# Starting a fused state-space and gated-MLP kernel tile by tile: first weights on two rings, ten f-tiles of the first token block ahead

## The chip, the cores and the metric

One NeuronCore of a Trainium2 chip. The metric is the device time of one execution in microseconds (us); lower is better. Every timed kernel is run several times, in rounds with the kernel before on the same chip.

## The reference, cut to what matters

```python
x = A_x                                   # (1, 2048, 576) bf16
xn = layernorm(x)                         # over the 576 columns
A  = s5(xn, Lambda, B, C, log_dt) + xn * Dskip    # linear recurrence over 2048 steps, 576 states
g, u = xn @ w_gate, xn @ w_up             # (2048, 576) @ (576, 4608), twice
Bm = (sigmoid(g) * u) @ w_down            # (2048, 4608) @ (4608, 576)
return x + A + Bm
```

Nearly all the work is matmul. The kernel cuts the 2048 tokens into four blocks of 512 (each four token tiles of 128 rows), and the 4608 columns f into 36 f-tiles of 128, twelve of them a "slot". A *group* is the gate and up product of one f-tile and one block: 18 matmuls of 512 columns. ScalarE (ACT) evacuates a group with a sigmoid and a cast, VectorE (DVE) multiplies the two into hT.

## The kernel before

TensorE needs normalized, transposed tokens (xT) and the first weights before it can do anything of its own; until then it multiplies zeros to keep its clock up. The first four token tiles come through the rings (queues of transfers) of SyncE (SP) and ACT, everything else through GpSimd (POOL).

```python
    def load_x(tt, eng, tag=None):
        if tag is None:
            xt = lnp.tile([P, D], BF16, name="xt", bufs=8)
        else:
            xt = hpool.tile([P, D], BF16, name="xt0", tag=tag, bufs=10)
        eng.dma_start(xt[:], x[tt * P:(tt + 1) * P, :])
        xts[tt] = xt
# ...
    def load_wgu(key, eng_g, eng_u):
        f0 = (key[0] % NC * (FC // FP) + key[1]) * FP * P
        w = wpool.tile([P, NH, FP * P], BF16, name="wgu", bufs=4)
        fs = slice(f0, f0 + FP * P)
        for (eng, rows, src) in ((eng_g, slice(0, H), B_w_gate), (eng_u, slice(H, P), B_w_up)):
            eng.dma_start(w[rows, :, :], src[:, fs].rearrange("(c p) f -> p c f", p=H))
        wgu_t[key] = w
# ...
    for tt in range(TT_B):
        load_x(tt, nc.sync if tt % 2 == 0 else nc.scalar)
    for pr in range(2):
        load_wgu((0, pr), nc.gpsimd, nc.gpsimd)
    for tt in range(TT_B, 2 * TT_B):
        load_x(tt, nc.gpsimd, "hst")
    dskip_rows = consts.tile([P, D], BF16, name="dskip_rows")
    nc.gpsimd.dma_start(dskip_rows[:], A_Dskip.partition_broadcast(P))
    for pr in range(2, 4):
        load_wgu((0, pr), nc.gpsimd, nc.gpsimd)
```

The first two groups, both on block 0, are done in halves of 256 columns, two token tiles to a half, transposed on TensorE:

```python
    for tt in range(2):
        ln_stats(tt)
        ln_std(0, tt, tt + 1)
    for tt in range(2):
        ln_recip(0, tt, tt + 1)
        ln_norm(tt, twice=False)
        start_transpose(tt)
    busy(20, P)
    start_copy(0, slice(0, NH), nc.scalar.copy)
    ln_stats(2)
    start_copy(1, slice(0, 5), nc.scalar.copy)
    ln_std(0, 2, 3)
    ln_stats(3)
    ln_std(0, 3, 4)
    start_copy(1, slice(5, NH), nc.vector.tensor_copy)
    for tt in range(2, TT_B):
        ln_recip(0, tt, tt + 1)
        ln_norm(tt, twice=False)
    start_groups[0].mms(slice(0, 2 * P))
    start_transpose(2)
    start_transpose(3)
    start_groups[1].mms(slice(0, 2 * P))
    for tt in range(2, TT_B):
        start_copy(tt, slice(0, 5), nc.scalar.copy)
        start_copy(tt, slice(5, NH), nc.vector.tensor_copy)
    for g in start_groups:
        g.mms(slice(2 * P, TB))
```

Then come six more groups of block 0, and then block 1, whose tokens are normalized on DVE in the background and transposed by DMA:

```python
            if slot == 0:
                order = [(f, 0) for f in range(2, 8)] + [(f, 1) for f in range(0, 8)]
                order += [(f, nb) for nb in range(2) for f in range(8, 12)]
# ...
            if slot == 0:
                run_groups([GateUp(slot, f, nb) for (f, nb) in order[:6]])
                catch_up_ln(1)
                order = order[6:]
                side_loads.extend([load_consts] + bt_loads)
            run_groups([GateUp(slot, f, nb) for (f, nb) in order])
```

## Time and profile before

| | before |
|---|---|
| median of 3 first runs (all 6 of the later comparison) | 509.69 us (509.9) |
| span of the profiled run, granted clock | 508.4 us, 1.00 |
| TensorE's first own matmul | 8.63 us |
| T2: first matmul on 512 columns, so both start groups' 256-column halves are done | 13.91 us |
| hole before block 1 | 1.79 us |
| first output matmul (pd) | 58.71 us |
| last matmul's start | 504.17 us |

Starts are counted from the beginning of the span. TensorE is busy without a gap from block 1's first group on, so whatever the start gains or loses appears unchanged at the end. The prediction shows TensorE's own lines. One more view: ACT's timeline of the kernel before. The columns are start, duration, engine (ACTq is its sequencer, issuing transfers), line, operation, output and input, count, and in brackets the idle time before and what ended it.

```profile
0.74 0.90 ACTq L139 DMA_DIRECT2D xt<-in_A_x_dram  x2
1.67 1.28 ACT L224 ACT_TABLE_LOAD   x1 [1.67 <-PEq L866]
4.69 0.29 ACT L224 ACTIVATE rstd<-mv,eps_t 128x1 f32<-128x1 f32 x1 [1.74 <-DVE mv L221]
```

ACT issues two token tiles, loads its square-root table, and then waits 1.74 us for DVE's statistics.

### The profile page before, as it was taken

The numbers are of one execution on the slowest core, as the hardware profiler recorded it, in microseconds if no ns is written. First come the engines' busy times: TensorE is split into PE (matmuls) and PEld (weight loads), VectorE is DVE, ScalarE is ACT, GpSimd is POOL, SyncE is SP. The second block draws the span as 40 slices with busy tenths as digits, with TensorE's granted clock in tenths as the row PEclk, the third lists the DMA queues.
The fourth block names the chain that finished last, engine by engine and source line by source line (L and its number), as shares of the span: only waits on it lengthen the run. The fifth ranks groups of instructions, "written<-read, shape, count | busy, mean of one in ns | idle before, by whom it ended". The sixth has DMA issues, their size and how long they took to land.

```text
span 508.4 us, 10667 instructions
## 1 busy us (share of the span) xinstructions
PE 500.6 (98%) x4536; PEld 292.6 (58%) x4536; DVE 323.5 (64%) x703; ACT 204.6 (40%) x368; POOL 96.6 (19%) x143
## 2 busy tenths in 40 slices
PE   8989999999999999999999999999999999999996
PEld 5445676444477444467764444774444774446775
DVE  6964999977888587868688667786675222221111
ACT  4757642556500756530016655005655005553000
POOL 6147430133110043110001231100431001300000
PEclk9999999999999999999999999999999999999999
DMA  8997997075220098342340662200753201600001
GB/s 208 172 170 143 235 194 125 2 164 122 57 57 25 1 170 153 76 107 69 73 104 3 163 141 48 46 24 1 150 122 81 48 25 38 172 1 4 33 25 36
DMA packets 42960, 45.60 MB, mean 90 GB/s; under 512 B 30496, under 2 KB 34336, under 8 KB 42912
## 3 DMA queue, kind: packets, MB, share of 16 engines
q0 software_dynamic: 12672, 34.23, 31.7%
q1 hardware_dynamic: 29808, 10.33, 10.2%
q8 instruction: 35, 0.57, 0.5%
q10 hardware_dynamic: 432, 0.37, 0.2%
q14 instruction: 13, 0.11, 0.1%
HBM read 34.36 MB, written 2.36 MB: 72 GB/s over the span
## 4 chain that ended last, share of the span: by engine, by line
PE 94%; DVE 3%; DMA 1%; ACT 1%; issue 0%
PE pgu L488 52%; PE pd L562 35%; PE pbu L517 7%; DVE bnst L220 1%; DMA xT<-xn 1%; DVE xn L240 1%; DMA xt<-in_A_x_dram 1%; ACT xT L737 0%; DVE acc L263 0%; PE ptr L734 0%; DVE mv L221 0%; DVE tmpxd L260 0%; DVE hT L497 0%; DVE ob L571 0%; DVE xn L245 0%
## 5 line engine op out<-in xcount | busy, mean ns | idle before, releaser
L488 PE MATMUL pgu<-xT,wgu 64*128 64x512 bf16 (+1 forms) x2628 | 283.7, 373 | 1.8 <-DMA xT<-xn 1.8
L488 PEld LDWEIGHTS <-wgu 64*128 64x128 bf16 x2628 | 130.0, 94 | 150.7 <-issue 2.5
L562 PE MATMUL pd<-wd,hT 128*128 128x288 bf16 x1152 | 144.6, 286 | 0.0
L494 ACT ACTIVATE sT<-pgu 128x512 bf16<-128x512 f32 x144 | 86.5, 600 | 119.4 <-PE pgu L488 109.7
L562 PEld LDWEIGHTS <-hT 128*128 128x128 bf16 x1152 | 112.2, 98 | 30.7 <-issue 0.8
L497 DVE TENSOR_TENSOR hT<-sT,uT 128x512 bf16<-128x512 bf16 x144 | 60.5, 421 | 100.0 <-ACT uT L495 99.8
L495 ACT CAST uT<-pgu 128x512 bf16<-128x512 f32 x144 | 84.1, 584 | 0.0
L151 POOL DMA_DIRECT2D wgu<-in_B_w_gate_dram x36 | 27.7, 769 | 227.7 <-PE pgu L488 207.7
L523 ACT COPY bure<-pbu 128x512 f32<-128x512 f32 x16 | 9.4, 585 | 104.3 <-PE pbu L517 88.5
L157 POOL DMA_DIRECT2D wd<-in_B_w_down_dram x36 | 26.4, 735 | 100.6 <-PE pd L562 99.5
L582 DVE TENSOR_TENSOR acc<-acc,pd 128x576 f32<-128x576 f32 x32 | 23.9, 750 | 24.1 <-PE pd L562 24.1
L579 DVE TENSOR_TENSOR ob<-acc,pd 128x576 bf16<-128x576 f32 x15 | 11.3, 754 | 40.9 <-PE pd L562 40.9
L517 PE MATMUL pbu<-xT,bt 64*128 64x512 bf16 x288 | 33.7, 376 | 0.0
L562 PEld LDWEIGHTS <-hst 128*128 128x128 bf16 x288 | 28.2, 98 | 7.1
L151 POOL DMA_DIRECT2D wgu<-in_B_w_up_dram x36 | 26.7, 742 | 1.5 <-issue 0.8
L562 PE MATMUL pd<-ctre,hst 128*128 128x288 bf16 x128 | 26.6, 286 | 0.0
L562 PE MATMUL pd<-ctim,hst 128*128 128x288 bf16 x128 | 26.6, 286 | 0.0
L432 DVE TENSOR_TENSOR_SCAN gre<-r,g0re,wrim 128x512 bf16<-128x512 f32 x20 | 25.5, 1277 | 0.1
L517 PEld LDWEIGHTS <-bt 64*128 64x128 bf16 x288 | 13.7, 94 | 17.1 <-issue 0.9
L439 DVE TENSOR_TENSOR_SCAN gim<-r,g0im,wrim 128x512 bf16<-128x512 f32 x16 | 20.4, 1276 | 0.0
L220 DVE BATCH_NORM_STATS2 bnst<-xt 128x6 f32<-128x288 bf16 x32 | 12.5, 433 | 2.4 <-DMA xt<-in_A_x_dram 2.4
L419 DVE TENSOR_TENSOR tq<-T,buim 128x512 bf16<-128x512 bf16 x20 | 13.7, 684 | 0.0
(113 smaller groups left out, 273.9 us busy)
## 6 DMA issues: line engine op xcount, KB each, us to landing
wgu<-in_B_w_gate_dram POOLq DMA_DIRECT2D x36, 288.0 KB, 4.4
wgu<-in_B_w_up_dram POOLq DMA_DIRECT2D x36, 288.0 KB, 5.1
wd<-in_B_w_down_dram POOLq DMA_DIRECT2D x36, 288.0 KB, 6.2
out_dram<-ob SPq DMA_DIRECT2D x15, 144.0 KB, 1.8
xt<-in_A_x_dram SPq DMA_DIRECT2D x10, 144.0 KB, 2.6
xt<-in_A_x_dram POOLq DMA_DIRECT2D x4, 144.0 KB, 7.2
bt<-ctre POOLq DMA_DIRECT2D x2, 288.0 KB, 6.9
bt<-ctim POOLq DMA_DIRECT2D x2, 288.0 KB, 7.8
```

The source lines that it names most:

```text
L151: eng.dma_start(w[rows, :, :], src[:, fs].rearrange("(c p) f -> p c f", p=H))
L157: nc.gpsimd.dma_start(wd[:], B_w_down[f0:f0 + FP * P, :].rearrange("(n p) d -> p n d", p=P))
L220: nc.vector.bn_stats(st[:, gi, :], xt[:, gi * DH:(gi + 1) * DH])
L432: nc.vector.tensor_tensor_scan(gre[:], r_bc, w[:, 0, :], g0re[:, col], ALU.mult, ALU.add)
L439: nc.vector.tensor_tensor_scan(gim[:], r_bc, w[:, 1, :], g0im[:, col], ALU.mult, ALU.add)
L488: nc.tensor.matmul(self.ps[:, gi, cols], w[rows, c, fs], xT[self.nb][rows, c, cols], start=c == 0, stop=c == NH - 1)
L494: nc.scalar.activation(sT[:], self.ps[:, 0, :], ACT.Sigmoid)
L495: nc.scalar.copy(uT[:], self.ps[:, 1, :])
L497: nc.vector.tensor_mul(h[:], sT[:], uT[:])
L517: nc.tensor.matmul(out, w, xT[self.nb][rows, c, ts_], start=c == 0, stop=c == NH - 1)
L562: nc.tensor.matmul(out, lhsT, rhs[:, a * DH:(a + 1) * DH], start=i == 0, stop=i == n - 1)
L582: nc.vector.tensor_add(halves(acc[:]), halves(acc[:]), pd[:, :, 0:DH])
```

## The change

The intent: get the first weights in sooner by using both fast rings for them at once; let TensorE begin when one token tile is ready instead of two; and put ten groups of block 0 ahead of block 1, so that block 1's input has two groups' time more. The transfers that are not needed at once are held back by a small memset. The diff, cut to its core:

```diff
-    def load_wgu(key, eng_g, eng_u):
+    def load_wgu(key, eng_g, eng_u, held=False):
...
-        w = wpool.tile([P, NH, FP * P], BF16, name="wgu", bufs=4)
+        if key == (0, 4):
+            w = consts.tile([P, NH, FP * P], BF16, name="wgu4", tag="T1")
...                                       # T1's own tile is made later, in tables()
+        else:
+            w = wpool.tile([P, NH, FP * P], BF16, name="wgu", bufs=4)
+        if held:
+            nc.vector.memset(w[:, 0, 0:2], 0.0)
...
     for tt in range(TT_B):
         load_x(tt, nc.sync if tt % 2 == 0 else nc.scalar)
-    for pr in range(2):
-        load_wgu((0, pr), nc.gpsimd, nc.gpsimd)
+    load_wgu((0, 0), nc.sync, nc.scalar)
     for tt in range(TT_B, 2 * TT_B):
-        load_x(tt, nc.gpsimd, "hst")
+        load_x(tt, nc.sync, "hst")
+    for pr in range(1, 3):
+        load_wgu((0, pr), nc.sync, nc.scalar)
...                                       # pairs 3 and 4 and dskip: on gpsimd, in load_behind(), called later
-    wgu_next = [4]
+    wgu_next = [5]
-            prefetch_wgu(pairs_done[0] + 4)
+            prefetch_wgu(max(pairs_done[0] + 4, min(pairs_done[0], 4) + 5))
-            if side_loads and i % 3 == 2:
+            if side_loads and i % 3 == 1:
...                                       # the start, shortened: four tiles, one at a time
-    start_groups[0].mms(slice(0, 2 * P))
-    start_transpose(2)
-    ...
-    start_groups[1].mms(slice(0, 2 * P))
+    start_norm(0)
+    start_transpose(0)
+    busy(14, P)
+    start_copy(0, CA, nc.scalar.copy)
+    ...
+    start_copy(0, CB, nc.scalar.copy)
+    ...
+    for g in range(2):
+        start_mms(g, 0, range(0, 5))
+    start_norm(1)
+    start_transpose(1)
+    ...                                   # each start_mms: 128 columns of one tile
...
-                order = [(f, 0) for f in range(2, 8)] + [(f, 1) for f in range(0, 8)]
-                order += [(f, nb) for nb in range(2) for f in range(8, 12)]
+                order = [(f, 0) for f in range(2, 10)] + [(f, 1) for f in range(0, 10)]
+                order += [(f, nb) for nb in range(2) for f in range(10, 12)]
...
+                bg.add(0.0, lambda: want_bu(0))
+                bg.add(0.0, lambda: want_bu(1))
                 for i in range(len(chain)):
                     queue_ssm(i)
-                want_bu(0)
-                want_bu(1)
```

More of the change, by code (lines that the diff above doesn't have):

```diff
@@ L163, with load_behind @@
         load_x(tt, nc.sync if tt % 2 == 0 else nc.scalar)
-    for pr in range(2):
-        load_wgu((0, pr), nc.gpsimd, nc.gpsimd)
+    load_wgu((0, 0), nc.sync, nc.scalar)
     for tt in range(TT_B, 2 * TT_B):
-        load_x(tt, nc.gpsimd, "hst")
+        load_x(tt, nc.sync, "hst")
+    for pr in range(1, 3):
+        load_wgu((0, pr), nc.sync, nc.scalar)
     dskip_rows = consts.tile([P, D], BF16, name="dskip_rows")
-    nc.gpsimd.dma_start(dskip_rows[:], A_Dskip.partition_broadcast(P))
-    for pr in range(2, 4):
-        load_wgu((0, pr), nc.gpsimd, nc.gpsimd)
+    def load_behind():
+        for pr in range(3, 5):
+            load_wgu((0, pr), nc.gpsimd, nc.gpsimd, held=pr == 3)
+        nc.gpsimd.dma_start(dskip_rows[:], A_Dskip.partition_broadcast(P))
     eps_t = consts.tile([P, 1], FP32, name="eps_t")
@@ L210, with ln_stats @@
     ln_count = [0]
-    def ln_stats(tt):
+    bnst = {}
+    def ln_stats(tt, parts=(0, 1)):
         nb, tl = divmod(tt, TT_B)
-        if tl == 0:
+        if tl == 0 and 0 in parts:
             mvs[nb] = lnp.tile([P, TT_B, nc.vector.BN_AGGR_DIM], FP32, name="mv")
@@ L217, in ln_stats @@
         xt = xts[tt]
-        st = lnp.tile([P, 2, BN], FP32, name="bnst")
-        for gi in range(2):
+        if 0 in parts:
+            bnst[tt] = lnp.tile([P, 2, BN], FP32, name="bnst")
+        st = bnst[tt]
+        for gi in parts:
             nc.vector.bn_stats(st[:, gi, :], xt[:, gi * DH:(gi + 1) * DH])
-        nc.vector.bn_aggr(mvs[nb][:, tl, :], st[:])
+        if 1 in parts:
+            nc.vector.bn_aggr(mvs[nb][:, tl, :], st[:])
     def ln_std(nb, t0, t1):
@@ L309 @@
     c512, s512 = sc4[:, 3, :], sc4[:, 2, :]
-    T1 = consts.tile([P, NU, TB], BF16, name="T1")
+    T1 = None
     T2 = consts.tile([P, NU, TB], BF16, name="T2")
@@ L378, in tables @@
     def tables(pt, part):
+        nonlocal T1
+        if T1 is None:
+            T1 = consts.tile([P, NU, TB], BF16, name="T1", tag="T1")
         sb_, cb_ = sc_tab[(pt, 0)], sc_tab[(pt, 1)]
@@ L481, in open, with mms @@
             self.ps = ps_pair("pgu")
-        def mms(self, cols=slice(0, TB)):
+        def mms(self, cols=slice(0, TB), cs=range(NH)):
             w = wgu_t[(self.slot, self.f // FP)]
             fs = slice((self.f % FP) * P, (self.f % FP + 1) * P)
-            for c in range(NH):
+            for c in cs:
                 for gi, rows in ((0, slice(0, H)), (1, slice(H, P))):
@@ L737, in start_copy, with start_mms, start_norm @@
         eng(xT_tile(0)[:, cs, tt * P:(tt + 1) * P], ptrs[tt % 2][:, cs, :])
-    for tt in range(2):
-        ln_stats(tt)
-        ln_std(0, tt, tt + 1)
-    for tt in range(2):
+    def start_mms(g, tt, cs=range(NH)):
+        start_groups[g].mms(slice(tt * P, (tt + 1) * P), cs)
+    CA, CB = slice(0, 5), slice(5, NH)
+    def start_norm(tt):
         ln_recip(0, tt, tt + 1)
         ln_norm(tt, twice=False)
-        start_transpose(tt)
-    busy(20, P)
-    start_copy(0, slice(0, NH), nc.scalar.copy)
-    ln_stats(2)
-    start_copy(1, slice(0, 5), nc.scalar.copy)
-    ln_std(0, 2, 3)
-    ln_stats(3)
-    ln_std(0, 3, 4)
-    start_copy(1, slice(5, NH), nc.vector.tensor_copy)
-    for tt in range(2, TT_B):
-        ln_recip(0, tt, tt + 1)
-        ln_norm(tt, twice=False)
-    start_groups[0].mms(slice(0, 2 * P))
-    start_transpose(2)
-    start_transpose(3)
-    start_groups[1].mms(slice(0, 2 * P))
-    for tt in range(2, TT_B):
-        start_copy(tt, slice(0, 5), nc.scalar.copy)
-        start_copy(tt, slice(5, NH), nc.vector.tensor_copy)
-    for g in start_groups:
-        g.mms(slice(2 * P, TB))
+    ln_stats(0)
+    ln_std(0, 0, 1)
+    ln_stats(1, (0,))
+    start_norm(0)
+    start_transpose(0)
+    busy(14, P)
+    start_copy(0, CA, nc.scalar.copy)
+    ln_stats(1, (1,))
+    ln_std(0, 1, 2)
+    start_copy(0, CB, nc.scalar.copy)
+    ln_stats(2, (0,))
+    for g in range(2):
+        start_mms(g, 0, range(0, 5))
+    start_norm(1)
+    start_transpose(1)
+    start_copy(1, CA, nc.scalar.copy)
+    for g in range(2):
+        start_mms(g, 0, range(5, NH))
+    load_behind()
+    ln_stats(2, (1,))
+    ln_std(0, 2, 3)
+    start_copy(1, CB, nc.scalar.copy)
+    ln_stats(3, (0,))
+    start_norm(2)
+    start_mms(0, 1)
+    start_transpose(2)
+    start_mms(1, 1)
+    ln_stats(3, (1,))
+    ln_std(0, 3, 4)
+    start_copy(2, CA, nc.scalar.copy)
+    start_copy(2, CB, nc.scalar.copy)
+    start_norm(3)
+    start_mms(0, 2)
+    start_transpose(3)
+    start_mms(1, 2)
+    start_copy(3, CA, nc.scalar.copy)
+    start_copy(3, CB, nc.vector.tensor_copy)
+    for g in range(2):
+        start_mms(g, 3)
     for tt in range(TT_B, 2 * TT_B):
@@ L813 @@
             if slot == 0:
-                run_groups([GateUp(slot, f, nb) for (f, nb) in order[:6]])
+                run_groups([GateUp(slot, f, nb) for (f, nb) in order[:8]])
                 catch_up_ln(1)
-                order = order[6:]
+                order = order[8:]
                 side_loads.extend([load_consts] + bt_loads)
```

## The prediction

> **What bounds the kernel now.** I read the page first, then the TensorE part of the timeline, then the waits of the first 35 us, the chain of the first 30 us, GpSimd's timeline and a table by stretches. From the page, the busy line of TensorE and the head of the chain that ended last:
>
> ```profile
> PE 500.6 (98%) x4536; PEld 292.6 (58%) x4536; DVE 323.5 (64%) x703; ACT 204.6 (40%) x368; POOL 96.6 (19%) x143
> ...
> PE 94%; DVE 3%; DMA 1%; ACT 1%; issue 0%
> ```
>
> TensorE is busy for 98% of the span, so all that can be won is its idle time and its work that isn't the kernel's. The timeline of TensorE alone (start, duration, what, then what ended the idle time before) shows where that lies:
>
> ```profile
> 1.25 4.16 PE L726 MATMUL pgu<-warm 128*128 128x512 bf16 x16 [1.25 <-DVE warm L178]
> 6.13 1.23 PE L734 MATMUL ptr<-ident,xn 128*64 128x128 bf16 x36 [0.72 <-DVE xn L245]
> 7.29 1.29 PE L726 MATMUL pgu<-warm 128*128 128x128 bf16 x20
> 8.63 1.16 PE L488 MATMUL pgu<-xT,wgu 64*128 64x256 bf16 x18
> 9.79 1.23 PE L734 MATMUL ptr<-ident,xn 128*64 128x128 bf16 x36
> 10.95 14.78 PE L488 MATMUL pgu<-xT,wgu 64*128 64x256 bf16 x162
> 27.52 20.68 PE L488 MATMUL pgu<-xT,wgu 64*128 64x512 bf16 x190 [1.79 <-DMA xT<-xn]
> ```
>
> Two things are to be seen. The first matmul of the kernel's own work is at 8.63 us. And there is one hole afterwards, 1.79 us before 27.52, where block 1's first group waits for block 1's transposed input. From 27.52 to the last matmul, at about 504.5, the waits of TensorE list nothing. So the change can only act before 27.52; a prediction is a prediction of when the same amount of group work has been done there. The table by stretches (us; busy of TensorE and of its weight loads, DVE, ACT, POOL; clock, DMA share, GB/s) cuts that part:
>
> ```profile
> 10.95:14.07 3.12, 3.12 (x60) 2.75 (x58) 2.58 (x8) 3.08 (x5) 2.31 (x6) 1.00 1.05 286
> 14.07:25.74 11.67, 11.65 (x108) 5.06 (x104) 11.06 (x25) 8.08 (x14) 0.17 (x3) 1.00 0.98 170
> 25.74:27.52 1.78, 0.00 (x1) 0.03 (x1) 1.75 (x5) 1.21 (x3) 0.00 (x0) 1.00 0.89 132
> ```
>
> 108 matmuls, six groups of 18, take 11.65 us: 1.94 us for a full group. The 162 matmuls from 10.95 are three half groups (256 columns) and these six, so a half group takes (14.78 - 11.65) / 3 = 1.04 us and the two start groups are done at **14.07** (call this time T2). Block 1 waits, in the chain, behind DVE and then a transfer:
>
> ```profile
> 16.93 3.21 DVE xn L240 x4
> ...
> 23.07 4.31 DMA xT<-xn
> ```
>
> Weights are nearly as late as the input. GpSimd's queue has eight transfers out and issues the next when an old one has landed; the ends of its waits give the landings of the first two weight pairs:
>
> ```profile
> 7.40 0.54 POOL L169 DMA_DIRECT2D dskip_rows<-in_A_Dskip_dram  x1 [0.67 <-DMA wgu<-in_B_w_gate_dram]
> 8.86 0.77 POOL L151 DMA_DIRECT2D wgu<-in_B_w_gate_dram  x1 [0.93 <-DMA wgu<-in_B_w_up_dram]
> 10.35 0.76 POOL L151 DMA_DIRECT2D wgu<-in_B_w_up_dram  x1 [0.72 <-DMA wgu<-in_B_w_gate_dram]
> ```
>
> So gate 0 came at about 7.4, up 0 at about 8.8 (first used at about 8.6), gate 1 at about 10.3: one 288 KB piece each 1.5 us, near 200 GB/s.
>
> **What the skill says.** The Trainium skill, page "DMA: Bandwidth & Descriptors", section "Issuing engines are not separate DMA queues": all queues end on the same 16 DMA engines, and issuing from several saves only the sequencer's time. The trace agrees: DMA share is 0.89 to 1.05 in all these stretches. Two rings will not bring more bytes; they only change the order. Same page, "Queues, rings and completion order": each engine takes turns between rings. No run here shows that yet, but it means that a load behind others in its ring also shares with the other rings. The page "Perfetto Trace Analysis", section "DMA Instruction — HWDGE (DVE, Sync)": the issuing sequencer is held until its descriptors are made. Here a token tile (128 rows) held ACT for about 0.43 us; a weight piece has 64 x 9 = 576 runs of 512 bytes, a cost which this trace doesn't show. The page "TensorE: Matmul & The Clock Gate", section "Back-to-back issue gap": at small N the weight load also sets the spacing. The trace agrees in kind: a pair at 512 columns takes 1.94/9 = 216 ns, at 256 columns 116 ns and not 108.
>
> **The change, part by part.**
>
> *Ten f-tiles ahead.* Block 1 starts after ten groups of block 0, not eight. Its input, ready at about 27.5, is then needed only at T2 + 8 x 1.943 = T2 + 15.54. The kernel before would have done the same ten groups' work by 27.52 + 2 x 1.943 = 31.41. So if there is no hole,
>
> change of time = T2(after) + 15.54 - 31.41 = T2(after) - 15.87.
>
> With T2 kept at 14.07 the gain is the whole hole, 1.8 us.
>
> *One tile at a time.* I walk the new order with the durations of before. Tile 0: stats 3.6 to 4.65, root 0.29 on ACT, reciprocal and norm to 5.6 (6.07 for the first pair before: 6.13 was its first transpose), 18 transposes 0.61 to 6.25, ACT's five-chunk copy 0.70 to 7.07. So first own matmuls at 7.1 instead of 8.63, if gate 0 and up 0 are there: 4 x 147 KB of tokens and 2 x 295 KB of weights, 1.18 MB at some 200 GB/s from about 1.5 us, is 7.4; I take 7.1 to 7.6. Tile 1's root now stands on ACT behind that copy (7.0 to 7.3), so its norm ends at 7.9 and its transposes at 8.55, where before both first tiles were transposed by 7.36. Tile 2: copy of tile 1 9.4, root 9.6, norm 10.2, transposes 10.4 to 11.0, as before. Tile 3: its transposes stand on TensorE behind group 0's piece of tile 2, which waits for both copies of tile 2 (about 12.3): 12.65 to 13.25, where before it was 11.0. Copies to 14.05, then two pieces.
>
> *128-column pieces.* 8 pieces take the place of 4 halves. If a pair of 128-column matmuls costs 65 to 90 ns (transposes went at 34 ns each, 68 a pair; half of 116 is 58), a piece is 0.6 to 0.8 us, 0.7 in the middle: 8 x 0.7 = 5.6 against 1.16 + 3.12 = 4.3, so 1.3 us more TensorE work. Lower bound for T2: 7.4 + 3 x 0.61 + 5.6 = 14.8. By the walk: 14.05 + 2 x 0.7 = 15.45. I take **T2 = 15.3**, from 14.3 to 16.5. The earlier first matmul (1.2 to 1.5 us) is thus more than paid back.
>
> *Two rings, held loads.* Order of bytes: tokens 0 to 3 and pair 0, then tokens 4 to 7 and pairs 1 and 2, with pairs 3 and 4 from about 8.5. Pair 1 is needed at T2. Before gate 1 is in, about 2.36 MB must come plus what the other rings take, some 0.5 MB. The transfers of before had moved 2.8 MB by 13.5 and 3.1 MB by 15 (summed from GB/s by slice). So gate 1 lands at 14 to 15: just in time.
>
> *Rest.* The memset (59 ns for the small ones now) and the shifted side loads lie off the path. The state matmuls are asked for after the tables instead of at once; TensorE has other groups to do and has no wait there now: 0.
>
> Sum: 15.3 - 15.87 = -0.6 us, by T2 between -1.6 and +0.6. From 509.69 this is 509.1; I lean 0.1 further, since my walk charges every wait in full: **509.0 us**.
>
> **The rivals.** (1) *The full intent*: pieces overlap well, T2 stays near 14, gain 1.8 us, 507.9. For it: all instruction counts on DVE and ACT stay nearly the same. Against it: the bound of 14.8 has no waits in it. More than 2 us needs T2 below 13.9; only much cheaper pieces would do that. (2) *ACT's queue becomes the wait*: three weight issues on ACT before its 1.28 us table load (at 1.67 now). At 0.5 us each the table is in at 4.4, before the root is asked for at 4.65; at 0.9 us it is 5.6 and everything moves by 1 us, T2 = 16.3, 510.1. If a full ring holds ACT until bytes have moved, it could be 2 us. (3) *Weights become the wait*: the ring of SP carries tokens 4 to 7 ahead of gate 1, and three rings share from 8.5. With equal shares gate 1 could come at 16 to 17: 509.8 to 510.8. (4) *The hole moves but stays*: DVE begins block 1's statistics after tile 3's last copy, 13.8 instead of 12.18, so block 1's input comes at about 27.5 + 1.6 = 29.1, later if pairs 3 and 4 crowd the transposing transfers. It is needed at 30.8: 1.7 us to spare, so most likely hidden. A late evacuation of a PSUM buffer at the fifth or sixth group is tight by some 0.4 us in the same walk and could add as much.
>
> **Range and chances.** Rivals 2 and 3 add up to 1 or 1.5 us, rival 1 takes away 1.1; run-to-run spread was 508.88 to 510.46. So 507.3 to 510.9 for 8 in 10. Two per cent is 10 us, more than the whole start phase can give: reaching it by gain would need nearly all of the first 8.6 us gone, by loss a stall that no row hints at.
>
> **What would show it.** Right: no wait on DMA in front of the first block-1 matmul; first own matmul at 7.1 to 7.8; the 128-column groups at 0.6 to 0.8 us for 18; the first 512-column group at about 15.3; the rest as before. Wrong: the first full group near 14 (the pieces overlap) or past 16.5 with ACT's issues or a weight transfer named in front; a wait before block 1 again; or any TensorE idle time after 31 us, which would mean that moving the state matmuls mattered.

## The result, and the profile after

| | before | after |
|---|---|---|
| median, 6 runs each | 509.9 us | 518.29 us (518.04 to 518.95) |
| span and granted clock of the profiled run | 508.4 us, 1.00 | 516.3 us, 0.993 |
| first root on ACT | 4.69 | 11.57 |
| first own matmul | 8.63 | 15.29 |
| T2 | 13.91 | 23.45 |
| hole before block 1 | 1.79 | none |
| first output matmul | 58.71 | 66.55 |
| last matmul's start | 504.17 | 512.63 |

The ratio is 1.0169, with an interval of 1.0155 to 1.0182: slower by 8.4 us, which is within 2% and far outside the predicted range. (A ratio is the mean time of one kernel's fast runs over that of the other's in the same rounds, so it is not quite the ratio of the medians that are quoted.) Executions over 1.5% slower than the fastest of the same kernel are left out of the means.

From the page of the kernel after, TensorE's busy line and the head of the chain that ended last:

```profile
PE 503.6 (98%) x4602; PEld 295.3 (57%) x4602; DVE 323.3 (63%) x702; ACT 205.9 (40%) x371; POOL 90.3 (17%) x133
...
PE 91%; DVE 4%; ACT 2%; DMA 2%; issue 1%; SPq 0%; ACTq 0%
```

TensorE's share still reads 98%, and its busy time grew by just 3 us. The share of the chain that is TensorE's fell from 94 to 91%: work of others now stands in front of it. The timeline of TensorE shows where:

```profile
1.25 4.62 PE L744 MATMUL pgu<-warm 128*128 128x512 bf16 x16 [1.25 <-DVE warm L188]
12.58 1.17 PE L752 MATMUL ptr<-ident,xn 128*64 128x128 bf16 x18 [6.72 <-DVE xn L260]
13.69 1.68 PE L744 MATMUL pgu<-warm 128*128 128x128 bf16 x14
15.29 0.80 PE L506 MATMUL pgu<-xT,wgu 64*128 64x128 bf16 x20
...
22.27 18.01 PE L506 MATMUL pgu<-xT,wgu 64*128 64x128 bf16 x188 [0.17 <-ACT xT L755]
```

The zeros end at 5.87, and then TensorE stands still for 6.72 us, until the first normalized tile. After 22.27 it runs through what was the hole. The name behind the wait, DVE's xn, is only the last link. ACT's timeline holds the cause:

```profile
1.68 8.57 ACTq L157 DMA_DIRECT2D wgu<-in_B_w_up_dram  x3
10.27 1.28 ACT L239 ACT_TABLE_LOAD   x1 [10.27 <-DMA wgu<-in_B_w_gate_dram]
11.57 0.29 ACT L239 ACTIVATE rstd<-mv,eps_t 128x1 f32<-128x1 f32 x1
```

Three issues of weights take ACT's sequencer from 1.68 to 10.25. The same view in two narrow windows (1.7 to 3 and 9.63 to 10.3) takes them apart:

```profile
1.68 1.38 ACTq L157 DMA_DIRECT2D wgu<-in_B_w_up_dram  x2
...
9.64 0.60 ACTq L157 DMA_DIRECT2D wgu<-in_B_w_up_dram  x1
```

Two issues took 1.38 us together and the third 0.60 us of its own. Between 3.06 and 9.64 ACT's sequencer did nothing at all: it waited 6.58 us before the third issue. This is no issue cost. The waits list it only at the table load behind it, and for its whole 10.3 us. The Trainium skill, page "Perfetto Trace Analysis", section "DMA Instruction — HWDGE (DVE, Sync)", has the semaphore wait of such an instruction ahead of its use of the descriptor generator, and the trace agrees in that the wait is not part of the 0.60 us. What ended it stands in the chain of the first 45 us (start, duration, what):

```profile
1.66 7.96 DMA wgu<-in_B_w_gate_dram
9.64 0.60 ACTq L157
10.24 0.03 issue
10.27 1.28 ACT L239
11.57 0.30 ACT rstd L239
```

The landing of gate 0, the first weight piece on the *other* ring, at 9.62 us, releases ACT. And SP's queue has the same kind of wait, one issue later in order (from the waits of SP's queue, first 40 us; total, times, longest):

```profile
SPq L157 <- DMA wgu<-in_B_w_up_dram: 2.6, 1, 2.6
```

The built program says why. In it, every transfer issued by SP or ACT reports its landing on one of eight completion semaphores (counters by which engines tell each other that something is done) that the two engines use together, in turn; a ninth transfer takes the first one's semaphore and is issued only when that first one has landed. GpSimd has eight of its own. This is how the program was built; no run here shows it to be a limit of the chip. The turn follows the order of the built program, which is not that of the source: up 1, twelfth in the source, is the eighth there. So the 13th issue is up 2, on ACT, and the fifth is gate 0; the 14th is gate 2, on SP, and the sixth is up 0. These are the two waits that the trace shows. The kernel before had only four transfers on these two rings at the start, so it did not get round to a ninth there. ACT, which needs its sequencer for the table load and the root, is the wrong engine to be held.

The clock adds to it. The table by stretches (busy of TensorE, its weight loads, DVE, ACT, POOL; clock, DMA share, GB/s):

```profile
12.50:13.75 1.25, 1.17 (x19) 1.00 (x20) 0.93 (x4) 0.00 (x0) 0.00 (x0) 0.50 1.17 189
13.75:15.36 1.61, 1.61 (x17) 1.41 (x18) 0.61 (x4) 1.36 (x3) 0.00 (x0) 0.50 0.43 75
15.36:16.09 0.73, 0.73 (x23) 0.63 (x24) 0.69 (x3) 0.00 (x0) 0.42 (x1) 0.92 0.05 11
```

After the 6.7 us idle the granted clock is 0.50 until about 15.5. The Trainium skill, page "TensorE: Matmul & The Clock Gate", section "Part 1: The HAM clock gate (the "warmup" mystery)", has a clock that falls to half when TensorE was idle over an activity window and comes back after about 3.4 us of work; the trace agrees in kind (6.7 us idle, half clock, full again after 2.9 us of work, from 12.58 to about 15.5).

Last, one small new wait at the first output matmuls (TensorE's timeline from 60 to 75 us):

```profile
66.55 2.87 PE L580 MATMUL pd<-wd,hT 128*128 128x288 bf16 x22
69.86 5.32 PE L580 MATMUL pd<-wd,hT 128*128 128x288 bf16 x42 [0.45 <-DVE hT L515]
```

So the account is: T2 later by 23.45 - 13.91 = 9.54, hole gone 1.79, new wait 0.45: +8.2, against +8.46 at the last matmul's start and +8.4 in the timed runs.

### The profile page after: what moved, and what is told of

The parts are those of the page before. It is cut to its first block, busy times and chain, and to the rows that moved or that the text cites. A ratio compares the mean times of both kernels' runs of the same rounds, so it can differ in the third digit from the quotient of the medians.

```text
span 516.3 us, 10801 instructions
## 1 busy us (share of the span) xinstructions
PE 503.6 (98%) x4602; PEld 295.3 (57%) x4602; DVE 323.3 (63%) x702; ACT 205.9 (40%) x371; POOL 90.3 (17%) x133
## 3 DMA queue, kind: packets, MB, share of 16 engines
q10 hardware_dynamic: 2208, 1.25, 1.0%
## 4 chain that ended last, share of the span: by engine, by line
PE 91%; DVE 4%; ACT 2%; DMA 2%; issue 1%; SPq 0%; ACTq 0%
PE pgu L506 50%; PE pd L580 34%; PE pbu L535 7%; DMA wgu<-in_B_w_gate_dram 2%; DVE sctab L336 1%; DVE bnst L234 1%; DVE rnd L335 1%; DVE ang L360 1%; PE ptr L752 0%; ACT L512 0%; ACT xT L755 0%; DVE hT L515 0%; ACT uT L513 0%; PE pgu L744 0%; ACT L339 0%
## 5 line engine op out<-in xcount | busy, mean ns | idle before, releaser
L506 PEld LDWEIGHTS <-wgu 64*128 64x128 bf16 x2700 | 132.1, 94 | 149.1 <-issue 2.3
L515 DVE TENSOR_TENSOR hT<-sT,uT 128x512 bf16<-128x512 bf16 x144 | 60.7, 423 | 100.3 <-ACT uT L513 100.1
L157 POOL DMA_DIRECT2D wgu<-in_B_w_gate_dram x33 | 25.4, 771 | 245.1 <-PE pgu L506 191.3
L535 PE MATMUL pbu<-xT,bt 64*128 64x512 bf16 x288 | 33.7, 377 | 0.0
L157 POOL DMA_DIRECT2D wgu<-in_B_w_up_dram x33 | 24.5, 741 | 0.6 <-DMA wgu<-in_B_w_up_dram 0.6
```

The lines of the kernel that those rows point to most:

```text
L506: nc.tensor.matmul(self.ps[:, gi, cols], w[rows, c, fs], xT[self.nb][rows, c, cols], start=c == 0, stop=c == NH - 1)
L515: nc.vector.tensor_mul(h[:], sT[:], uT[:])
L535: nc.tensor.matmul(out, w, xT[self.nb][rows, c, ts_], start=c == 0, stop=c == NH - 1)
```

## The experiments

Theory: ACT is held by a completion semaphore that comes round after eight transfers (about 6.9 us of the loss), the cold clock adds about 1, and the tile-by-tile start costs the rest. Rivals: ACT's ring has no room for a fifth transfer, so ACT is held until bytes have moved; the weights themselves come late and would have held TensorE anyway; the ten f-tiles or the shifted background work cost time later. Twelve kernels ran; all gave the right result. Two more builds went to no chip: the change with the two state matmuls asked for at once as before (the schedule deadlocks while it is being built), and ten f-tiles ahead without the shifted side loads (reading a tile before it was written). So these two parts of the diff belong to the ten f-tiles and are no tuning of their own.

### u2_on_sp: take the held issue off ACT

```diff
-    for pr in range(1, 3):
-        load_wgu((0, pr), nc.sync, nc.scalar)
+    load_wgu((0, 1), nc.sync, nc.scalar)
+    load_wgu((0, 2), nc.sync, nc.sync)
```

> The changed kernel with one issue moved: up 2 from ACT's queue to SP's. My theory: ACT was held from 3.05 to 9.64 us by this one issue, which waits for a completion semaphore that gate 0 (landed at 9.62) still holds. Then ACT's table load is over at about 4.4 us, the first root starts at about 4.7 instead of 11.57, and the first own matmul waits for gate 0 only, at about 9.7 instead of 15.29. T2 comes down from 23.6 to 16.5 to 17.5 and the time to about 511.5 us (510.5 to 512.5). Rival: the three rings and late weights are the cause and ACT's wait only stood in front of them; then T2 stays above 21 us and the time above 515.5 us.

Measured: 514.52 us (4 runs; before 510.06), ratio 1.0098 [1.0071, 1.0125]. ACT's timeline:

```profile
3.08 1.28 ACT L239 ACT_TABLE_LOAD   x1 [3.08 <-issue]
4.73 0.29 ACT L239 ACTIVATE rstd<-mv,eps_t 128x1 f32<-128x1 f32 x1 [0.37 <-DVE mv L236]
```

With the third issue gone from ACT the root is back at 4.73 and T2 falls from 23.45 to 17.4. The time fell by less, because of TensorE's waits (total, times, longest):

```profile
PE pgu L506 <- DMA wgu<-in_B_w_up_dram: 1.6, 1, 1.6
PE pgu L506 <- DMA wgu<-in_B_w_gate_dram: 1.4, 1, 1.4
...
PE pd L580 <- DVE hT L515: 1.0, 1, 1.0
```

Gate 0 now holds the first own matmul to 8.86, and up 2, issued on SP at 9.47 and landed only at 23.2, holds TensorE for 1.58 us at 23.25. I had left that second one out. The mechanism was as expected, the size was not.

### x_on_pool: the same five transfers on ACT, fewer on the two rings together

```diff
     for tt in range(TT_B, 2 * TT_B):
-        load_x(tt, nc.sync, "hst")
+        load_x(tt, nc.gpsimd, "hst")
```

> The changed kernel with token tiles 4 to 7 issued by GpSimd instead of SP; ACT keeps its three weight issues. There are then ten transfers on SP and ACT at the start instead of fourteen, and up 2 waits for the semaphore of token tile 1 (landed at about 3.5 us), not of gate 0. My theory (completion semaphores): ACT is free at about 4.1, the table is in at 5.4, the root starts then, gate 0 lands before 8.5 because no tokens share its ring; T2 15 to 17 and 509.5 to 511.5 us. Rival (ring capacity: an issue is held until its ring has room, whatever the semaphores): ACT is still held until 8 to 10 us, as its ring has the same five transfers, and the time stays at 515 to 518.5 us.

Measured: 515.68 us (512.96 to 517.23, 4 runs, with granted clocks of 0.993 to 0.999), ratio 1.0106 [1.0066, 1.0146]; span of the profiled run 511.1. ACT's timeline:

```profile
1.67 2.60 ACTq L157 DMA_DIRECT2D wgu<-in_B_w_up_dram  x3
4.30 1.28 ACT L239 ACT_TABLE_LOAD   x1 [4.30 <-DMA xt<-in_A_x_dram]
```

ACT issues the very same five transfers (two tokens, three weights) and is free at 4.27, not 10.25. A ring too small for them would have held it here too, so the rival of the full ring is out. With four transfers fewer in the turn, up 2 is the tenth and has to wait for the second only, an early token tile: the releaser named is a token tile. The time was expected lower: gate 0 and up 0 came at about 9.1 and 9.6, T2 was 17.77, and some runs had a colder clock. The median lies in the rival's range of 515 to 518.5, so the time alone would not decide; ACT's row does. The spread makes this run good for the mechanism and poor for the time.

### ten_ahead: the ten f-tiles alone, on the kernel before

The diff's parts for ten f-tiles (tile wgu4 in T1's place, pair 4 on GpSimd behind pair 3, the prefetch rule, the two orders of ten, the state matmuls and side loads), with the start and the rings as before.

> The kernel before with the ten f-tiles ahead alone (with the buffer, side loads and order of the state matmuls that it needs), its start as it was. My theory: T2 stays at 14.1, the 1.79 us hole in front of block 1 closes, minus up to 0.4 us for a new wait of the first output matmul on hT: 508.1 to 508.6 us. Rival: the fifth pair's load makes block 1's transposed input later, or DVE falls behind so far that a wait of the same size opens elsewhere: 509.5 us or more.

Measured: 509.14 us (the median of three fast runs, 508.93, 509.14 and 510.5; a fourth run was slow, 517.72), ratio 0.9991 [0.9967, 1.0016]. TensorE's timeline:

```profile
11.18 45.93 PE L494 MATMUL pgu<-xT,wgu 64*128 64x256 bf16 x450
57.05 2.87 PE L568 MATMUL pd<-wd,hT 128*128 128x288 bf16 x22
60.34 9.85 PE L568 MATMUL pd<-wd,hT 128*128 128x288 bf16 x79 [0.42 <-DVE hT L503]
```

One run of 450 matmuls: the hole is gone, and the first output matmul starts at 57.05 instead of 58.71. A wait of 0.42 for hT has come in behind it. The profiled span is 1.3 us shorter (507.1), the fast runs 0.5 us on the mean, within the interval. This part of the change shows no harm; its gain is at the edge of what can be timed.

### ten_pieces: the 128-column pieces alone

```diff
-    start_groups[0].mms(slice(0, 2 * P))
+    start_groups[0].mms(slice(0, P))
+    start_groups[0].mms(slice(P, 2 * P))
...                                    # the same for group 1 and for the second halves
```

> As the run with ten f-tiles ahead alone, but each of the four half groups cut into two 128-column pieces, nothing else. In the changed kernel 18 matmuls of 128 columns took 0.62 to 0.68 us. My theory: 8 x 0.65 in place of 4 x 1.04 (+0.12 for the first) is 0.9 us more TensorE work on the path: 0.6 to 1.1 us slower than the run beside it. Rival: the pieces fit between waits, 0 to 0.3 us.

Measured: 510.13 us, ratio 1.0004 [0.9983, 1.0024], against 0.9991 for ten_ahead: 0.7 us more on the mean, as expected, but the intervals overlap. TensorE's timeline:

```profile
9.09 1.18 PE L494 MATMUL pgu<-xT,wgu 64*128 64x128 bf16 x36
```

36 matmuls of 128 columns, two pieces back to back, took 1.18 us; the 18 of 256 columns that they replace took 1.16. From the first own matmul to T2, all own matmuls keep TensorE busy for 4.38 us in both runs. So a piece costs no more than its share when its input is there, and the 0.9 us of the expectation are not in the trace; the narrower matmul as such is not what makes the tile-by-tile start long. The time itself is inconclusive: T2 was 14.87 against 14.14, but in that profile the first 36 transposes took 1.67 us (1.23 in the kernel before), so that the first own matmul came 0.45 later.

### keep_warm: the clock's part

```diff
-    busy(10, TB)
+    busy(36, TB)
```

> The changed kernel with 26 more warm-up matmuls of 512 columns before the first transposes (wrong in nothing: their sums are overwritten). ACT is held as before, so the root stays at about 11.6 us. My theory: of the 8.2 us by which the first own matmul came later than my walk, 6.9 are ACT's wait and about 1.1 to 1.3 are the clock, granted at 0.50 from 12.5 to 15.4 us after 6.7 us of idle TensorE. Then the first own matmul moves from 15.3 to about 14.0 and the time falls by 1.0 to 1.4 us, to about 517.0. Rival: the clock costs nothing, as the copies bound this stretch: 518.0 to 518.5.

Measured: 517.04 us (516.25 to 517.42), ratio 1.0138 [1.0123, 1.0153], 1.25 us less than after; before in this batch 510.0. TensorE's timeline:

```profile
12.58 0.69 PE L752 MATMUL ptr<-ident,xn 128*64 128x128 bf16 x18 [1.62 <-DVE xn L260]
13.20 0.96 PE L744 MATMUL pgu<-warm 128*128 128x128 bf16 x14
14.09 0.73 PE L506 MATMUL pgu<-xT,wgu 64*128 64x128 bf16 x20
```

The first tile is transposed at the same moment, 12.58, but in 0.69 us instead of 1.17; T2 is 22.35, earlier by 1.10. ACT's lines are the same as in the kernel after, root at 11.57. So the cold clock is 1.1 us of T2, and no more.

### u_early: the same transfers on the same rings, in another order

```diff
-    load_wgu((0, 0), nc.sync, nc.scalar)
+    for pr in range(3):
+        load_wgu((0, pr), nc.sync, nc.scalar)
     for tt in range(TT_B, 2 * TT_B):
         load_x(tt, nc.sync, "hst")
-    for pr in range(1, 3):
-        load_wgu((0, pr), nc.sync, nc.scalar)
```

> The changed kernel with its fourteen transfers on SP and ACT in another order of the program: all three weight pairs first, then token tiles 4 to 7, on the same rings. Up 2 is then the tenth and takes the completion semaphore of token tile 1 (landed near 3.4 us). My theory: ACT is free at about 4.3, the root starts at 5.6, pair 2 comes in time (no wait of TensorE for up 2, where the run with up 2 on SP had 1.6 us), gate 0 lands between 7.5 and 9.5; T2 16 to 17.3 and 510.5 to 512.5 us. Rival (ACT is held by its ring, or weights are late whatever the order): first own matmul past 11 us or a new wait for weights of over 1 us, 514 us or more.

Measured: 511.72 us (511.14 to 511.82), ratio 1.0032 [1.0016, 1.0049]. ACT's timeline:

```profile
1.67 2.74 ACTq L157 DMA_DIRECT2D wgu<-in_B_w_up_dram  x3
4.45 1.28 ACT L238 ACT_TABLE_LOAD   x1 [4.45 <-DMA xt<-in_A_x_dram]
5.74 0.29 ACT L238 ACTIVATE rstd<-mv,eps_t 128x1 f32<-128x1 f32 x1
```

TensorE's first own matmul:

```profile
8.78 0.73 PE L505 MATMUL pgu<-xT,wgu 64*128 64x128 bf16 x20 [0.45 <-DMA wgu<-in_B_w_gate_dram]
```

This is the decisive run. Each engine issues the same transfers as in the kernel after; only the four token tiles now stand behind the weights. Up 2 is the tenth issue and reuses the second token tile's semaphore, and 6.6 us of the 8.4 are gone. A limit on how many transfers the two rings may have out together, whichever they are, is not it either: token tile 6, the 13th here, was issued at 8.75, when gate 0 had landed (8.73), although up 0 had landed at 7.87. The first own matmul is at 8.78, after 0.45 us for gate 0, and T2 at 17.13, with no wait for up 2. What remains follows the sum: 17.13 - 13.91 - 1.79 + 0.5 (hT) = +1.9, timed +1.7. And it sets the price of the tile-by-tile start: from first own matmul to T2 it takes 8.35 us, where the kernel before takes 13.91 - 8.63 = 5.28. In this stretch TensorE is busy with own matmuls for 5.77 us (4.12 before) and with transposes for 2.08 (1.23), overlapping a little, and idle for 0.91 (0). As the cut alone left the 4.38 us of ten_ahead as they were (ten_pieces), the extra time goes with pieces that come one by one between transposes and copies; no run separates this further.

### early_consts: move the small constants' loads to win the hT wait too

The wait of 0.42 in ten_ahead comes from DVE, which is behind: with ten groups first, two groups fewer are left before the output matmuls to take in the angle tables of the state part. Loading the constants earlier should spread them.

```diff
+                side_loads.extend([load_consts])
                 run_groups([GateUp(slot, f, nb) for (f, nb) in order[:8]])
                 catch_up_ln(1)
                 order = order[8:]
-                side_loads.extend([load_consts] + bt_loads)
+                side_loads.extend(bt_loads)
```

> Ten f-tiles ahead alone, with the loads of the small constants issued during block 0 and not after it. In the run with ten f-tiles ahead, and in all runs with that order, the first output matmul waits 0.4 to 1.0 us for hT behind the angle tables on DVE, because these start only a fixed number of groups after that load. My theory: that wait goes, 0.3 to 0.6 us less than ten f-tiles ahead alone: 508.3 to 509.2 us. Rival: the earlier change of ACT's table delays evacuations during block 0 and TensorE waits there instead: same or slower.

Measured: 509.52 us (509.44 to 509.63), ratio 0.9992 [0.9978, 1.0007]. TensorE's timeline:

```profile
34.88 23.49 PE L494 MATMUL pgu<-xT,wgu 64*128 64x512 bf16 x216 [1.13 <-ACT uT L501]
```

The hT wait is gone, and one of 1.13 us for an evacuation has come at 34.9: from 28.8 to 33.7 us ACT did no evacuation, for it loaded two tables (1.28 us each) and waited 1.91 us for DVE between them. The rival was right.

### best2: early_consts, with pair 0 alone on the two rings

```diff
-    for pr in range(2):
-        load_wgu((0, pr), nc.gpsimd, nc.gpsimd)
+    load_wgu((0, 0), nc.sync, nc.scalar)
+    load_wgu((0, 1), nc.gpsimd, nc.gpsimd)
```

> As the run before it in this list, with weight pair 0 alone moved to the rings of SP and ACT (six transfers on these two in all, none waits). The up issue holds ACT for about 0.7 us, the table is in at 3.7, before the root at 4.6. My theory: the first own matmul waits no more for up 0 (8.9 in the profile of ten f-tiles ahead) and starts with the copies at 8.6: 0.2 to 0.5 us less, 508.0 to 508.9 us. Rival: ACT's later table load or slower token tiles delay the root, 509.5 us or more.

Measured: 515.38 us (512.48 to 516.25, clocks 0.992 to 0.997), ratio 1.0097 [1.0065, 1.0129]. TensorE's timeline:

```profile
10.98 1.24 PE L494 MATMUL pgu<-xT,wgu 64*128 64x256 bf16 x18 [2.33 <-DMA wgu<-in_B_w_gate_dram]
12.16 2.13 PE L740 MATMUL ptr<-ident,xn 128*64 128x128 bf16 x36
```

My expectation failed. ACT was free (root at 4.53), but gate 0 landed at about 10.9, while GpSimd's transfers had been issued beside it. TensorE waited 2.33 us and then ran cold: 36 transposes in 2.13 us where the kernel before takes 1.23; the granted clock in these was 0.50. The Trainium skill, page "DMA: Bandwidth & Descriptors", section "Queues, rings and completion order", has the engines take turns between the rings; the trace agrees as far as it goes: 238 GB/s moved from 5 to 10.9 us, most of it not what was wanted first.

### consts_mid: the constants a little later

The same edit as early_consts, with the load after the eighth of these groups instead of the second.

> Ten f-tiles ahead alone, with the loads of the small constants after the eighth of the groups on block 0 (in the run with ten f-tiles ahead alone after the tenth, where the first output matmul waited 0.4 us for hT; in the run with early constants after the second, where TensorE waited 1.1 us for an evacuation behind ACT's table load). My theory: neither wait is there, T2 stays at 14.1 to 14.3 and the 1.79 us hole is closed: 1.3 to 1.8 us less than the kernel before, 508.2 to 508.8 us. Rival: the wait only moves again, 509.3 us or more.

Measured: 509.31 us (509.08 to 510.65, 6 runs; before 509.95), ratio 0.9989 [0.9973, 1.0005]. The evacuation's wait is gone and the one for hT is back, 0.91 us at 60.7. Expectation missed: the wait has only moved.

### p0_alone: pair 0 on the rings, with nothing beside it

On consts_mid: pair 0 as in best2, and all of GpSimd's transfers held by a memset of two columns until tile 0's statistics are done (about 4.8 us).

```diff
+    def load_behind():
+        load_wgu((0, 1), nc.gpsimd, nc.gpsimd, held=True)
+        ...                            # tokens 4 to 7, dskip, pairs 2 to 4
         ln_stats(tt)
         ln_std(0, tt, tt + 1)
+        if tt == 0:
+            load_behind()
```

> As the run beside it, with weight pair 0 alone on the rings of SP and ACT, and every transfer of GpSimd held until the first tile's statistics are done (about 4.7 us). In the run with pair 0 on the rings and GpSimd's transfers free, gate 0 landed at about 10.9 and TensorE waited 2.3 us for it. My theory: gate 0 was late because the transfers issued on GpSimd at the same time took most of the engines' turns; held, gate 0 and up 0 land by 7.8, no wait for weights before the first own matmul at 8.6, 508.0 to 509.0 us. Rival: a weight pair on these rings lands after 8.8 us whatever else is in flight; then the first own matmul waits and the time is 509.5 us or more.

Measured: 509.71 us (509.07 to 509.99), ratio 0.9989 [0.9976, 1.0003]. TensorE's timeline:

```profile
8.53 1.16 PE L498 MATMUL pgu<-xT,wgu 64*128 64x256 bf16 x18
...
30.05 27.37 PE L498 MATMUL pgu<-xT,wgu 64*128 64x512 bf16 x252 [0.62 <-ACT uT L505]
```

The same two transfers on the same two rings now are there before 8.53, with no wait for them: the traffic beside them had made them late in best2. T2 is 13.71, earlier than in the kernel before by 0.2, and it is taken back by 0.62 for an evacuation and 0.96 for hT. The time was expected lower, at 508 to 509; it falls in the rival's range, but not for the rival's reason, since the weights were in time.

### ten_angle and p0_angle: slow DVE's background work down

```diff
-            bg.add(1.35, lambda pt=pt, which=which: angle(pt, which))
+            bg.add(1.8, lambda pt=pt, which=which: angle(pt, which))
```

> Ten f-tiles ahead alone, with the angle tables entered in the background queue at a cost of 1.8 us each instead of 1.35 (one takes DVE 1.60 us beside 0.42 us for hT, together more than the 1.94 us of a group). My theory: the wait of the first output matmul for hT (0.4 us with ten f-tiles ahead alone) is DVE's backlog of these tables; spread thinner, it goes, and the gain of the closed hole stays whole: 508.0 to 508.9 us, 0.3 to 0.5 us under that run's 509.1. Rival: the tables, now later, delay the state chain, and a wait opens in later stages: 509.5 us or more.

> The run with pair 0 alone on the rings and GpSimd held (first own matmul 8.53 us, waits of 0.96 us for hT and 0.62 us for an evacuation), with the same cost for the angle tables. My theory: the 0.96 us wait goes, the other may stay: 508.2 to 509.2 us. Rival: as for the run beside it, 509.5 us or more.

Measured: ten_angle (on ten_ahead) 512.43 us, ratio 1.0038 [1.0022, 1.0054]; p0_angle (on p0_alone) 510.78 us, 1.0014 [1.0002, 1.0026]; before 510.07. TensorE's waits in ten_angle:

```profile
PE pd L568 <- DVE hst L471: 2.0, 1, 2.0
```

The wait for hT is gone in both, and a wait of 2.0 us for the state part (hst) is there at about 256 us in both: the slower tables make the recurrence late, as the rival had it; this chain is argued, only the wait is shown. (Four of ten_angle's six runs also had a somewhat lower clock, 0.995 to 0.997, so its 512.43 is no clean measure of that wait.) The rival was right in both. No version that was tried clearly beats the kernel before; ten_ahead, early_consts, consts_mid and p0_alone lie at 0.999 with intervals that include 1. Whether some placement of the background work wins the whole hole stays open.

## Why the prediction was wrong

**The bound, right.** The start was all that counted, and T2 sets the time. The formula "T2(after) - 15.87" gives 23.45 - 15.87 = +7.6 for the measured T2, or +7.75 with T2 before read in the same way (13.91, not the derived 14.07). With the hT wait of 0.45 that is +8.2; the timed runs have +8.4, and 0.2 us stays unplaced.

**T2, wrong by 8 us.** The walk had 15.45. The measured 23.45 is that walk with two terms put in: ACT's root at 11.57 instead of 4.65 (6.92) and the cold clock (1.10 by keep_warm), 15.45 + 6.92 + 1.10 = 23.47. (The walk's steps hold small hand-over times that it doesn't list: 0.70 after 6.25 is 6.95, it wrote 7.07.)

**The failed step: rival 2, "ACT's queue becomes the wait".** It named the right engine and the right three issues, and took them for an issue cost: "If a full ring holds ACT until bytes have moved, it could be 2 us." The issue cost was inside its range, 0.60 to 0.70 us each, and cost little: in u_early all three are made by 4.41, a short wait for a token tile included, and the root stands at 5.74, about 1 us after the walk's 4.65; at the first own matmul this is hidden by the wait for gate 0. What holds ACT is not the ring's room (x_on_pool) but the landing of the fifth transfer, whose completion semaphore the 13th takes over. The prediction had this very rule in front of it: "GpSimd's queue has eight transfers out and issues the next when an old one has landed." I did not ask whether the other two rings have such a rule, counted together. Counting would have been enough: 14 transfers against eight, the 13th on the engine that owes the first root (the 14th by the source's order, behind up 0), and its semaphore owed by a weight piece, which by the prediction's own figure lands no earlier than about 7.4. The prediction's own sign, a first full group "past 16.5 with ACT's issues or a weight transfer named in front", came true; only its size was not in any rival.

**Gate 0's landing, wrong but hidden.** "1.18 MB at some 200 GB/s from about 1.5 us, is 7.4" counts only the bytes that are wanted; by 9.6 us 2.0 MB had been moved. It landed at 9.62 in the kernel after, at 8.7 to 9.1 in u_early, u2_on_sp and x_on_pool, and at about 10.9 in best2; of the kernels with pair 0 on the rings, only the one with GpSimd's transfers held had it in time for 8.53. (Its "about 7.4" for the kernel before is the start of GpSimd's next issue; by the semaphore's record in the trace, gate 0 had landed at 7.1 and up 0 at 8.6.) In the kernel after the lateness costs nothing directly, since xT comes later still; it costs by being what ACT waits for. In the first three of those other runs it is part of the remainder (0.45 to 1.4 us).

**The clock, not in the walk.** The walk took each duration from a warm kernel. Here an idle time of 6.72 us in front of TensorE brought half clock with it, and so did 2.33 us in best2; 1.62 us in keep_warm did not.

**The tile-by-tile start, right in length.** "The earlier first matmul is thus more than paid back": from the first own matmul to T2 the walk had 15.45 - 7.1 = 8.35 us; u_early took 8.35 and the kernel after 8.16; that the first agrees to the hundredth is luck. Pieces of 0.6 to 0.8 us were 0.62 to 0.68 where they ran through, and 0.86 to 0.89 where the second of their two copies came late. The 1.3 us more TensorE work were 1.65 in u_early (5.77 against 4.12), but not by the narrower matmul, as the prediction had it (ten_pieces).

**The ten f-tiles, right in the main.** The hole closed in every kernel that has them. Not foreseen: DVE's background work gets two groups less before the output matmuls, which gives back 0.4 to 1.0 us there. I had said that idle time after 31 us would mean that the state matmuls' move mattered. The runs point to DVE instead, since moving the constants' loads moves the wait (early_consts); that the state matmuls have no part in it can't be shown, as their move can't be undone alone.

The loss by runs: 1.25 us by the clock (keep_warm); 6.6 by the order of issue, the clock's part included (u_early); what then is left over the kernel before is 1.7, and over ten_ahead about 2 (by the ratios), for the tile-by-tile start and the later weights.

## What to carry to other kernels

Before moving transfers to another ring, write down all issues of the engines that share completion semaphores, in the order of the built program, and see, for each that comes after the semaphores have all been used once (here from the ninth on), which landing it waits for and what else the waiting engine owes at that moment; put no issue that can be held on an engine which is about to do the first step of the chain. Two rings alone did not bring weight pair 0 sooner (whole at 8.7 to 10.9 us, against 8.6 before); with the other transfers held back it was there by 8.2 (p0_alone). A piece of work placed earlier takes its room from background work that was there, so look for where that work comes out.

## What the Trainium skill lacked or had wrong

- No page says that an issue can be held because its completion semaphore is still owed by an earlier transfer, on another engine's ring. In this program SP and ACT take turns over eight, and ACT stood for 6.58 us before an issue of 0.60. The page "DMA: Bandwidth & Descriptors" asks for one semaphore per in-flight slot (section "Why a DMA increments its semaphore by 16 and not by 1") but not what that does to the next issue. This belongs there, with the hint that here ACT's row in the trace showed it only as a stretch between two issues.
- Same page, section "Issuing engine by pattern": issues from SP and ACT are generally faster than GpSimd's, without saying what is faster. In the kernel after the issue of a weight piece itself is (0.60 to 0.74 us against 0.73 to 0.89). The landing was not: gate 0 came at 7.1 by GpSimd in the kernel before, and at 8.7 to 10.9 on SP's ring beside other traffic (8.2 with GpSimd's held).
- Same page, section "Queues, rings and completion order": the turns between rings are stated, their size for a kernel is not. One 288 KB piece issued at 1.66 us landed at 9.62 (after) and at about 10.9 (best2).
- The page "Perfetto Trace Analysis" gives no issue cost for a piece of many short runs: 576 runs of 512 bytes held ACT for 0.60 to 0.70 us, a token tile of 128 rows for 0.45.
